# Attention and two feed-forward layers on one core: another way to transpose queries and keys, and other places for the weight splits

## The chip, the core and the metric

The kernel runs on one core of a Trainium2 chip, in one launch. The core has a matrix engine (TensorE; PE in the rows, with its weight loads as PEld), a vector engine (VectorE, DVE), a scalar engine (ScalarE, ACT), a general engine (GpSimd, POOL) and a queue engine (SyncE, SP) that here issues nearly all transfers. Each engine works through its own instructions in the order in which the program gives them, and waits for other engines by semaphores. The metric is the device time of one execution, in microseconds (us). The median of three runs of the kernel before is 856.53 us (856.2 to 856.91).

## The reference

Three stages in float32, each fed by the one before (cut to what matters):

```python
# q, k, v: [4, 8, 576, 64]; a query sees itself and the 63 tokens before it
scores = scale * (q @ k.transpose(0, 1, 3, 2))
mask = (rel >= 0) & (rel < 64)
attn = softmax(where(mask, scores, -1e9))
x = (attn @ v).transpose(0, 2, 1, 3).reshape(2304, 512)
# 8 experts of 288 tokens each, chosen greedily by the logits of x @ w_gate
out[mask_e] = maximum(x[mask_e] @ w1[e], 0) @ w2[e]     # 512 -> 1024 -> 512
# gated layer; its three weights come in float64
g = x @ w_gate2                                          # 512 -> 1536
y = (g * sigmoid(g) * (x @ w_val)) @ w_out               # 1536 -> 512
```

## The kernel before, in words

**Attention.** The 8 heads are taken as 4 pairs, head hp and head hp + 4, so that 128 partitions hold 64 values of d of two heads. A unit is a window of 64 queries of one pair; a pair has 9 units, all 16 pairs (4 batches) have 144, and a group is four units that follow each other, so there are 36 groups. The loop over the groups is written out as a software pipeline: in step i the matrix engine makes the scores of group i (`scores`, a mask matmul and a float32 matmul for each unit), transposes the probabilities of group i - 3 (`transposed`) and multiplies those of group i - 5 with the values (`values`); the vector engine takes the maxima of group i, the scalar engine the exponentials of group i - 1 (`exponents`), and GpSimd divides by the sums (`norms`, `pn`). The scalar engine then moves the results out (`out_x`).

Queries and keys are needed with d on the partitions. Before the change the transfers bring 32 tokens and 32 values of d to a quadrant of 32 partitions (`load_qk`: pieces of 32 float32, 128 bytes), and the vector engine transposes 32 by 32 blocks (`prep_k`, `prep_q`: one instruction for the keys of a pair, two for the queries). Only the first two pairs come in rows of eight tokens and are transposed on the matrix engine (`rows`). Values of the block before are copied to the lower 64 partitions by the vector engine and GpSimd (`prep_v`). A small planner gives each of these steps the latest group at which it may come (`steps`, `todo`, `vtodo`, `loads`).

**Routing.** Six rounds of `step`: matrix engine counts (`cnt`), a test on the vector engine (`sat`), two small matmuls (`low`, `tot`), and then the vector engine and GpSimd make the next candidates (`M`, `U`, `below`, `Us`, `u`, `G`). Beside each round three tiles of x are transposed and stored in DRAM, and `Stream.split` prepares the first expert weights on GpSimd.

**Weights.** All weights are used as two float32r parts whose sum is exact: the scalar engine copies the raw tile to the high part (`whi`), and another engine subtracts it for the low part (`wlo`), half a tile of 128 x 1024 at a time. For the experts' weights one half is subtracted on the vector engine and the other on GpSimd. `need` asks for five tiles ahead, with nine buffers for each part. The gated layer's float64 weights are put together as float32 by their bits: one square on the scalar engine and four vector instructions for half a tile (`convert`, tiles `t` and `sq`), 36 halves in all, loaded and stored by `convert_move`.

**Experts.** For each of 8 experts and 8 steps f: `first` (12 matmuls of 288 columns), the second product of the step before (12 more), up to three pieces of the next expert's rows transposed, and three parts of `convert` (two where a piece was transposed). All conversion is done before the last expert (`convert_rest`).

**Gated layer.** Three groups of 768 tokens, 12 steps f each, two blocks a step: 24 matmuls of 384 columns a block, and then 18 matmuls of 512 columns for the step before (`second`). Two PSUM banks (`psg`) alternate between the gate's product and the value's.

The order of the work on each engine is the order in which the program emits it; nothing reorders it later.

Of the kernel before, what the change touches and what calls it, by code (L numbers as in the profile page):

```python
# [7 lines left out]
F32 = mybir.dt.float32  # L8
# [13 lines left out]
class Stream:  # L22
    """Weights: loaded in float32, split on chip into two float32r parts whose sum is exact."""

    def __init__(self, ctx, tc):
        self.nc = tc.nc
        self.raw = ctx.enter_context(tc.tile_pool(name="wraw", bufs=4))
        self.todo, self.raws, self.parts = [], [], {}
        self.nload = self.nsplit = 0
# [8 lines left out]
    def load(self, upto):  # L38
        while self.nload < min(upto, len(self.todo)):
            key, src = self.todo[self.nload]  # L40
            t = self.raw.tile([128] + list(src.shape[1:]), F32, name="wraw")
            self.nc.sync.dma_start(t, src)
            self.raws.append(t)
            self.nload += 1

    def split(self, upto, engine=None):
        upto = min(upto, len(self.todo))
        self.load(upto + 4)
        while self.nsplit < upto:
            key, _ = self.todo[self.nsplit]  # L50
            t = self.raws[self.nsplit]
            h = self.hi.tile(list(t.shape), F32R, name="whi")
            lo = self.lo.tile(list(t.shape), F32R, name="wlo")
            for s in range(2):
                if len(t.shape) == 3 and t.shape[1] % 2 == 0:
                    m = t.shape[1] // 2
                    sl = (slice(None), slice(s * m, s * m + m))
# [3 lines left out]
            self.parts[key] = (h, lo)  # L61
            self.nsplit += 1


class Kernel:
# [29 lines left out]

    def attention(self, ctx):
# [10 lines left out]
        NR = 3  # L107
        raw_p, kt_p, v_p = pool("raw", NR), pool("kt", 3), pool("vw", 8)
# [9 lines left out]
        nc.gpsimd.iota(iq, pattern=[[2, 64]], base=0, channel_multiplier=-1)  # L118
        nc.vector.tensor_scalar(gt, iq, 0.0, None, op0=OP.is_gt)
# [7 lines left out]
        vone = one.tile([128, 1, 1, 1], F32, name="vone")  # L127
        nc.vector.memset(vone, 1.0)
# [4 lines left out]
        NQ, KL, VL = 5, 2, 5  # L133
        qbds = [one.tile([128, NC, 64, 2], F32, name=f"qbd{i}") for i in range(NQ)]
        for i in range(NQ):
            for s in range(2):
                nc.gpsimd.memset(qbds[i][64 * s:64 * s + 64, :, :, 1 - s], 0.0)
# [4 lines left out]
        # A unit is a window of 64 queries of one pair of heads, hp and hp + HP. A group is four units.  # L142
# [4 lines left out]
        raw, kt, vw = {}, {}, {}  # L147

        def load_qk(b, name, j):
            """On the partitions of a quadrant 32 tokens, and 32 of d."""  # L150
            src = self.k if name == "k" else self.q
            raw[name, b, j] = raw_p.tile([128, 2, S // 32, 32], F32, name="raw" + name)
            for s in range(2):
                for dh in range(2):
                    p0, h = 64 * s + 32 * dh, HP * s + 2 * j
                    nc.sync.dma_start(
                        raw[name, b, j][p0:p0 + 32].rearrange("p h t d -> p (h t) d"),
                        src[b, h:h + 2, :, 32 * dh:32 * dh + 32].rearrange("h (t p) d -> p (h t) d", p=32))

        def load_rows(name, h):  # L160
            src = self.k if name == "k" else self.q
            t = v_p.tile([128, NC, 2, D], F32, name="vw")
            raw[name, h] = t[0:72, 0:8].rearrange("p c s d -> p (c s d)").rearrange("p (s x) -> p s x", s=2)
            for s in range(2):
                nc.sync.dma_start(raw[name, h][:, s], src[0, HP * s + h].rearrange("(p t) d -> p (t d)", t=8))

        def load_v(b, hp):
            vw[b, hp] = v_p.tile([128, NC, 2, D], F32, name="vw")
            for s in range(2):
                nc.sync.dma_start(vw[b, hp][64:128, :, s, :], self.v[b, HP * s + hp].rearrange("(c p) d -> p c d", p=64))  # L170

        def rows(name, h):
            """Keys or queries of pair h of the first batch, transposed on the tensor engine; a partition has 8 tokens,
            and two at a time are transposed."""
            p, n = (ps_t, "ps_t") if name == "k" else (ps_o, "ps_o")
            if name == "k":
                dst = kt[0, 0][:, h].rearrange("r (p t e) -> r e t p", t=4, e=2)
            else:
                dst = qbd(0, h).rearrange("r c i s -> r (c i) s").rearrange("r (p t e) s -> r s e t p", t=4, e=2)
            for s in range(2):  # L180
                sl = slice(64 * s, 64 * s + 64)
                ps = p.tile([128, 4, 72], F32, name=n)
                for t in range(4):
                    nc.tensor.transpose(ps[:, t, :], raw[name, h][:, s, 128 * t:128 * t + 128], self.ident[0:72, 0:72])
                for e in range(2):
                    x = ps[64 * e:64 * e + 64]
                    if name == "k":
                        nc.scalar.activation(dst[sl, e], x, AF.Copy)
                    else:
                        nc.vector.tensor_copy(dst[sl, s, e], x)  # L190

        def prep_k(b, hp):
            if hp % 2 == 0:
                kt[b, hp // 2] = kt_p.tile([128, 2, S], F32, name="kt")
            if b == 0 and hp < 2:
                rows("k", hp)
                return
            nc.vector.transpose(kt[b, hp // 2][:, hp % 2], raw["k", b, hp // 2][:, hp % 2].rearrange("p t d -> p (t d)"))

        def prep_q(b, hp, s):  # L200
            if b == 0 and hp < 2:
                if s == 0:
                    rows("q", hp)
                return
            r = raw["q", b, hp // 2][:, hp % 2].rearrange("p (i e) d -> p i (e d)", e=2)
# [982 lines left out]
```

## Time and profile before

| what | value |
| --- | --- |
| median of 3 runs | 856.53 us |
| span of the profiled execution (first to last instruction) | 854.2 us |
| TensorE busy / VectorE busy | 796.9 us (93%) / 542.7 us (64%) |
| ScalarE busy / GpSimd busy | 383.4 us (45%) / 225.3 us (26%) |
| DMA packets, those under 512 bytes | 137931, 88896 |
| DMA moved | 119.50 MB |
| attention, first scores to the last group's mask matmul | 10.16 to 114.13 us |
| routing, first to sixth count | 125.87 to 154.41 us |
| experts, first product to the gated layer's first | 173.14 to 400.61 us |
| gated layer, to the last scatter | 400.61 to 849 us |

The profile gives no time of its own for the profiled execution but its span; what lies around the span is taken as the difference to the median of the runs, 2.3 us. The busy share is an average over these stages, and each of them has another limit, so that they have to be read one by one. A row of the timeline holds start, duration, engine, line, operation, output, inputs, shape, and in brackets the idle time before it and what ended that. A row of a group holds the same for all instructions of a line, with count, total, mean in ns, and the idle time before.

### The profile page before, as it was taken

The numbers are of one execution on the slowest core, as the hardware profiler recorded it, in microseconds if no ns is written. First come the engines' busy times: TensorE is split into PE (matmuls) and PEld (weight loads), VectorE is DVE, ScalarE is ACT, GpSimd is POOL, SyncE is SP. The second block draws the span as 40 slices with busy tenths as digits, with TensorE's granted clock in tenths as the row PEclk, the third lists the DMA queues.
The fourth block names the chain that finished last, engine by engine and source line by source line (L and its number), as shares of the span: only waits on it lengthen the run. The fifth ranks groups of instructions, "written<-read, shape, count | busy, mean of one in ns | idle before, by whom it ended". The sixth has DMA issues, their size and how long they took to land.

```text
span 854.2 us, 14581 instructions
## 1 busy us (share of the span) xinstructions
PE 796.9 (93%) x5411; PEld 738.6 (86%) x5411; DVE 542.7 (64%) x1014; ACT 383.4 (45%) x980; POOL 225.3 (26%) x263
## 2 busy tenths in 40 slices
PE   5879895499999999999999999999999999999996
PEld 4668774299999999999999999999999999999996
DVE  5868888789999999976443444554344454433422
ACT  4777875356555665666322323433222343221311
POOL 6765745544455444440000000020000002000002
PEclk9999997599999999999999999999999999999998
DMA  9999935679999998855311222241122224101001
GB/s 141 137 142 144 195 113 177 186 243 312 290 318 307 302 315 287 285 187 174 99 29 46 74 74 74 75 149 35 41 74 74 75 74 148 43 32 50 1 1 74
DMA packets 137931, 119.50 MB, mean 140 GB/s; under 512 B 88896, under 2 KB 105280, under 8 KB 137856
## 3 DMA queue, kind: packets, MB, share of 16 engines
q1 hardware_dynamic: 134976, 109.09, 47.2%
q0 software_dynamic: 2880, 9.44, 3.6%
q8 instruction: 44, 0.72, 0.4%
q14 instruction: 31, 0.25, 0.1%
HBM read 99.63 MB, written 18.87 MB: 139 GB/s over the span
## 4 chain that ended last, share of the span: by engine, by line
issue 36%; PE 24%; DVE 16%; POOL 2%; ACT 1%; DMA 0%; POOLq 0%; DVEq 0%; ACTq 0%
PE psg L983 13%; DVE wlo L60 6%; PE pso L983 5%; PE psa L983 3%; PE psw L983 3%; DVE t L940 2%; DVE hl L973 2%; DVE t L938 2%; POOL out_dram L1123 2%; DVE t L936 2%; DVE t L942 1%; DVE xt L976 1%; ACT whi L58 0%; PE psw L1015 0%; DMA w<-t 0%
## 5 line engine op out<-in xcount | busy, mean ns | idle before, releaser
L983 PE MATMUL psg<-y,whi 128*128 128x384 f32 x1152 | 223.1, 336 | 0.0
L983 PEld LDWEIGHTS psg<-y,whi 128*128 128x128 f32 x1152 | 201.6, 188 | 0.0
L1123 POOL DMA_INDIRECT out_dram<-orow,idx x18 | 17.3, 963 | 443.5 <-ACT orow L1121 271.6
L983 PE MATMUL pso<-whi,p 128*128 128x512 f32 x432 | 133.3, 390 | 0.0
L60 DVE TENSOR_TENSOR wlo<-wraw,whi 128x512 fp32r<-128x512 f32 x167 | 129.6, 820 | 4.5 <-ACT whi L58 4.1
L58 ACT ACTIVATE whi<-wraw 128x512 fp32r<-128x512 f32 x236 | 130.4, 620 | 0.1
L60 POOL TENSOR_TENSOR wlo<-wraw,whi 128x512 fp32r<-128x512 f32 x69 | 100.0, 1459 | 103.4 <-ACT whi L58 40.2
L1100 DVE TENSOR_TENSOR sg<-sg,psg 128x384 f32<-128x384 f32 x72 | 39.9, 554 | 131.7 <-ACT sg L1099 131.7
L983 PE MATMUL psg<-y,wlo 128*128 128x384 f32 x576 | 123.4, 336 | 0.0
L1105 ACT ACTIVATE p<-sg 128x384 fp32r<-128x384 f32 x72 | 37.8, 525 | 152.7 <-DVE sg L1103 150.5
L983 PEld LDWEIGHTS psg<-y,wlo 128*128 128x128 f32 x576 | 102.5, 188 | 2.8 <-DVE sg L1100 0.2
L1099 ACT ACTIVATE sg<-psg 128x384 f32<-128x384 f32 x72 | 35.4, 491 | 147.0 <-PE psg L983 147.0
L983 PEld LDWEIGHTS pso<-whi,p 128*128 128x128 f32 x432 | 80.6, 188 | 14.5
L983 PE MATMUL pso<-wlo,p 128*128 128x512 f32 x216 | 84.2, 390 | 0.0
L983 PE MATMUL psa<-hl,whi 128*128 128x288 f32 x256 | 78.4, 306 | 5.2 <-DVE hl L973 4.8
L1103 DVE TENSOR_TENSOR sg<-sg,psg 128x384 f32<-128x384 f32 x72 | 39.9, 554 | 66.5 <-PE psg L983 66.2
L983 PE MATMUL psw<-xt,whi 128*128 128x288 f32 x512 | 78.4, 295 | 0.0
L983 PE MATMUL psa<-hh,whi 128*128 128x288 f32 x256 | 75.4, 295 | 0.0
L983 PE MATMUL psa<-hh,wlo 128*128 128x288 f32 x256 | 75.4, 295 | 0.0
L983 PEld LDWEIGHTS psw<-xt,whi 128*128 128x128 f32 x512 | 71.3, 188 | 0.0
L1106 DVE TENSOR_TENSOR p<-sg,p 128x384 fp32r<-128x384 f32 x72 | 40.2, 559 | 42.6 <-ACT p L1105 42.0
L245 ACT ACTIVATE pp<-ps_s,nm 128x128 f32<-128x128 f32 x144 | 51.0, 369 | 26.8 <-DVE nm L238 24.6
(179 smaller groups left out, 1157.9 us busy)
## 6 DMA issues: line engine op xcount, KB each, us to landing
wraw<-in_moe_w_dram SPq DMA_DIRECT2D x64, 512.0 KB
wraw<-w SPq DMA_DIRECT2D x54, 512.0 KB
w<-t SPq DMA_DIRECT2D x36, 256.0 KB
raw<-in_moe_w_gate_dram SPq DMA_DIRECT2D x12, 512.0 KB
raw<-in_moe_w_val_dram SPq DMA_DIRECT2D x12, 512.0 KB
raw<-in_moe_w_out_dram SPq DMA_DIRECT2D x12, 512.0 KB
vw<-in_v_dram SPq DMA_DIRECT2D x32, 144.0 KB
xrows<-row SPq DMA_DIRECT2D x18, 256.0 KB
```

What stands on the lines that cost most here:

```text
L58: self.nc.scalar.activation(h[sl], t[sl], AF.Copy)
L60: eng.tensor_tensor(lo[sl], t[sl], h[sl].bitcast(F32), op=OP.subtract)
L245: nc.scalar.activation(PP[g][:, u, :], ps[:, u, :], AF.Exp, bias=nm[:, u:u + 1], scale=scale, accum_out=SM[g][:, u:u + 1])
L936: nc.vector.tensor_scalar(t, hi, 0x07FFFFFF, 3, op0=OP.bitwise_and, op1=OP.logical_shift_left)
L938: nc.vector.scalar_tensor_tensor(t, hi, -0x40000000, t, op0=OP.bitwise_and, op1=OP.bitwise_or)
L983: self.nc.tensor.matmul(acc, x, y, start=start and i == 0, stop=stop and i == len(seq) - 1)
L1099: nc.scalar.activation(sg, pg, AF.Sigmoid)
L1100: nc.vector.tensor_tensor(sg, sg, pg, op=OP.mult)
L1103: nc.vector.tensor_tensor(sg, sg, pv, op=OP.mult)
L1105: nc.scalar.activation(p[0][:, sl], sg, AF.Copy)
L1106: nc.vector.tensor_tensor(p[1][:, sl], sg, p[0][:, sl].bitcast(F32), op=OP.subtract)
L1123: d = nc.gpsimd.indirect_dma_start(out=self.out, out_offset=bass.IndirectOffsetOnAxis(ap=self.idx[:, 6 * g + t:6 * g + t + 1], axis=0), in ...
```

## The change

Queries and keys of all pairs now come in rows of two tokens (128 float32, 512 bytes: `load_rows`) on 72 partitions, and the matrix engine transposes them, four transposes into one PSUM bank for each of two heads and for q and k (`prep`). The keys leave PSUM in two copies on the scalar engine, the queries in two on the vector engine, each copy writing every second float32. The scores' operands lie head by head rather than interleaved, and the mask is made accordingly. Values of the block before are copied by a transfer on the chip (`copy_v`). `out_x` moves from the scalar to the vector engine in the loop. The scores have two PSUM banks instead of three, the transposes three instead of two.

No weight is split on GpSimd any more. `Stream.half` splits half a tile, on the scalar and vector engines, and stands in `step` between the counts and `sat` in the first six rounds; after the routing `split(6)` takes the place of six conversion parts. `need` asks for four tiles ahead, with seven buffers. `convert` is called for 10 parts an expert and goes on through the last expert and into the gated layer, four parts after each block; a tile is loaded only once it is stored (`limit`). The comments that the change deletes are left out here.

```diff
+        self.limit = lambda: len(self.todo)
-        self.hi = ctx.enter_context(tc.tile_pool(name="whi", bufs=9))
-        self.lo = ctx.enter_context(tc.tile_pool(name="wlo", bufs=9))
+        self.hi = ctx.enter_context(tc.tile_pool(name="whi", bufs=7))
+        self.lo = ctx.enter_context(tc.tile_pool(name="wlo", bufs=7))
...
-    def split(self, upto, engine=None):
-        upto = min(upto, len(self.todo))
-        self.load(upto + 4)
...
-                self.nc.scalar.activation(h[sl], t[sl], AF.Copy)
-                eng = engine or (self.nc.gpsimd if s and key[0] in ("w1", "w2") else self.nc.vector)
-                eng.tensor_tensor(lo[sl], t[sl], h[sl].bitcast(F32), op=OP.subtract)
...
+    def half(self):
+
+        if self.nsplit == len(self.todo):
+            return
+        self.load(self.nsplit + 5)
...
+        sl = (slice(None), slice(self.nhalf * m, self.nhalf * m + m))
+        self.nc.scalar.activation(h[sl], t[sl], AF.Copy)
+        self.nc.vector.tensor_tensor(lo[sl], t[sl], h[sl].bitcast(F32), op=OP.subtract)
+        self.nhalf = 1 - self.nhalf
+        self.nsplit += not self.nhalf
...
+        NR, NQ, NV, VL = 3, 4, 6, 5
...
-        ps_s, ps_t, ps_o, ps_l = pool("ps_s", 3, PS), pool("ps_t", 2, PS), pool("ps_o", 2, PS), pool("ps_l", 1, PS)
+        ps_s, ps_t, ps_o, ps_l = pool("ps_s", 2, PS), pool("ps_t", 3, PS), pool("ps_o", 2, PS), pool("ps_l", 1, PS)
...
+        def load_rows(name, b, hp):
+
             src = self.k if name == "k" else self.q
-            raw[name, b, j] = raw_p.tile([128, 2, S // 32, 32], F32, name="raw" + name)
+            t = raw[name, b, hp] = raw_p.tile([72, 2, 4, 2 * D], F32, name="raw" + name)
             for s in range(2):
...
+                nc.sync.dma_start(t[:, s], src[b, HP * s + hp].rearrange("(t p e) d -> p t (e d)", p=72, e=2))
...
+        def copy_v(b, hp):
+
+            nc.sync.dma_start(vw(b, hp)[0:64, 1:NC], vw(b, hp)[64:128, 0:NC - 1])
+
+        def prep(name, b, hp, s):
+
+
+            ps = ps_t.tile([128, 4, 72], F32, name="ps_t")
+            for t in range(4):
+                nc.tensor.transpose(ps[:, t, :], raw[name, b, hp][:, s, t], self.ident[0:72, 0:72])
...
+            dst = dst.rearrange("r c (m e) -> r e c m", e=2)
+            for e in range(2):
+                x = ps[64 * e:64 * e + 64].rearrange("r t p -> r (t p)").rearrange("r (c m) -> r c m", c=NC)
+                if name == "k":
+                    nc.scalar.activation(dst[:, e], x, AF.Copy)
+                else:
+                    nc.vector.tensor_copy(dst[:, e], x)
...
-                out_x(i - VL - 1)
+                out_x(i - VL - 1, True)
             take(i)
             if i >= 1:
                 norms(i - 1)
-            for a in vtodo.get(i, ()):
-                prep_v(*a)
...
             def beside(i):
-                self.st.split(i, self.nc.gpsimd)
                 self.store_rows(3)
                 self.convert_move()
...
                 mm(cnt, G[:, c, :], bl[:, c, :], start=c == 0, stop=c == NT - 1)
+            if it < first:
+                self.st.half()
             nc.vector.tensor_scalar(self.sat[0:32], cnt[:, 0:NE], cnt[:, NE:NE + 1], 0.5 - CAP,
...
+        if self.halves:
+            st.limit = lambda: 8 * NE + self.stored // 2 if self.stored < len(self.halves) else len(st.todo)
 
     def need(self, key):
-        self.st.split(self.order[key] + 5)
+        self.st.split(self.order[key] + 4)
...
         self.convert_move()
-        self.convert(6)
+        self.st.split(6)
...
-                n = 3
                 if todo and f % 2 == 0:
                     transposed(*todo.pop(0))
-                    n = 2
-                if e < NE - 1:
-                    self.convert(n)
-                elif f in (1, 4):
+                self.convert(2 if f % 4 == 3 else 1)
+                if e == NE - 1 and f in (1, 4):
                     self.ready(f // 4)
...
+                self.convert_move()
                 block(g, f, p, 0)
+                self.convert()
...
+                self.convert_move()
                 block(g, f, p, 1)
+                self.convert()
```

What this does to the order on the engines is shown at three places. The first is one group in the middle of the attention on the matrix engine, before the change: mask and scores (`ps_s`), transposes of the probabilities (`ps_t`), products with the values (`ps_o`).

```order
L225 LDWEIGHTS identb
L225 MATMUL ps_s<-mask,identb 128x512
L229 MATMUL ps_s<-kt,qbd_143 128x128 x4
L262 MATMUL ps_t<-ident,pn 128x128 x4
L278 MATMUL ps_o<-pt,vw 64x64 x8
```

And a group of the changed kernel at the same stage, `rawq` and `rawk` being the rows of queries and keys of a later pair.

```order
L206 LDWEIGHTS identb
L206 MATMUL ps_s<-mask,identb 128x512
L210 MATMUL ps_s<-kt,qbd_146 128x128 x4
L243 MATMUL ps_t<-ident,pn 128x128 x4
L259 MATMUL ps_o<-pt,vw_156 64x64 x8
L184 MATMUL ps_t<-ident,rawq 128x72 x4
L184 MATMUL ps_t<-ident,rawk 128x72 x4
```

Eight transposes of 72 rows have come to the end of the group; the vector engine's 32 by 32 transposes are gone from its own order.

The second place is the vector engine in two steps of an expert, before: `hl` is the low part of the hidden layer, `wlo` that of a weight, `xt` that of the next expert's rows, and `t` are conversion parts.

```order
L973 SCALAR_TENSOR_TENSOR hl<-psw,hh 128x288
L976 TENSOR_TENSOR xt_5961<-psw,xt_5960 128x4x64
L942 SCALAR_TENSOR_TENSOR t_6015<-sq_6016,t_6015 128x512
L936 TENSOR_SCALAR t_6068<-raw_5941 128x512
L973 SCALAR_TENSOR_TENSOR hl<-psw,hh 128x288
L60 TENSOR_TENSOR wlo<-wraw,whi 128x512
L938 SCALAR_TENSOR_TENSOR t_6068<-raw_5941,t_6068 128x512
L940 SCALAR_TENSOR_TENSOR t_6068<-raw_5941,t_6068 128x512
L942 SCALAR_TENSOR_TENSOR t_6068<-sq_6069,t_6068 128x512
L60 TENSOR_TENSOR wlo<-wraw,whi 128x512
```

The same engine in two steps of an expert of the changed kernel.

```order
L933 SCALAR_TENSOR_TENSOR hl<-psw,hh 128x288
L936 TENSOR_TENSOR xt_6270<-psw,xt_6269 128x4x128
L896 SCALAR_TENSOR_TENSOR t_6393<-raw_1757,t_6393 128x512
L933 SCALAR_TENSOR_TENSOR hl<-psw,hh 128x288
L60 TENSOR_TENSOR wlo<-wraw,whi 128x512 x2
L898 SCALAR_TENSOR_TENSOR t_6393<-raw_1757,t_6393 128x512
L60 TENSOR_TENSOR wlo<-wraw,whi 128x512 x2
```

Four halves of weights stand where two stood, the other two having been on GpSimd, and two conversion parts where five stood.

The third place is the vector engine in the gated layer, where the second step of the first group ends and the third begins, in the changed kernel: `sg` and `p` belong to the block, `t` to the conversion, `wlo` to the next three weight tiles.

```order
L1056 TENSOR_TENSOR sg<-sg,psg 128x384
L1059 TENSOR_TENSOR sg<-sg,psg 128x384
L1062 TENSOR_TENSOR p_9195<-sg,p_9194 128x384
L894 TENSOR_SCALAR t_9273<-raw_9153 128x512
L896 SCALAR_TENSOR_TENSOR t_9273<-raw_9153,t_9273 128x512
L898 SCALAR_TENSOR_TENSOR t_9273<-raw_9153,t_9273 128x512
L900 SCALAR_TENSOR_TENSOR t_9273<-sq_9274,t_9273 128x512
L60 TENSOR_TENSOR wlo<-wraw,whi 128x512 x6
L1056 TENSOR_TENSOR sg<-sg,psg 128x384
```

Before the change no conversion stands here: only the six halves came between the blocks.

## Rows read from the trace of the kernel before

**Rows 1.** Windows: length, then busy us (count) of PE, PEld, DVE, ACT, POOL.

```profile
core 0 of [0], span 854.2 us
66.46:80.30 13.84, 13.74 (x178) 12.03 (x174) 13.34 (x39) 12.89 (x60) 10.68 (x13) 1.00 1.23 141
173.14:400.61 227.47, 222.26 (x1629) 213.81 (x1630) 212.79 (x298) 137.57 (x284) 101.80 (x73) 1.00 0.86 276
```

**Rows 2.** Timeline, PE, attention: first scores, then mask matmuls of three groups.

```profile
10.16 2.04 PE L229 MATMUL ps_s<-kt,qbd 128*128 128x128 f32 x8 [2.44 <-ACT kt L188]
...
66.46 0.39 PE L225 MATMUL ps_s<-mask,identb 128*128 128x512 bf16 x1
...
80.30 0.39 PE L225 MATMUL ps_s<-mask,identb 128*128 128x512 bf16 x1
...
114.13 0.38 PE L225 MATMUL ps_s<-mask,identb 128*128 128x512 bf16 x1
```

**Rows 3.** Groups by line, 0 to 160 us: query transposes and copies out of PSUM.

```profile
L206 DVE STREAM_TRANSPOSE qbd<-rawq 64x576 f32<-64x576 f32 x28 | 21.6, 771 | 12.4 <-DMA rawq<-in_q_dram 12.0
...
L188 ACT ACTIVATE kt<-ps_t 64x288 f32<-64x288 f32 x8 | 5.5, 684 | 4.6 <-PE ps_t L184 4.5
...
L190 DVE COPY qbd<-ps_o 64x288 f32<-64x288 f32 x8 | 5.2, 646 | 1.6 <-PE ps_o L184 1.5
```

**Rows 4.** Timeline, PEld, 13 to 16 us: eight transposes of keys.

```profile
14.31 0.58 PEld L184 LDWEIGHTS ps_t<-ident,vw 72*128 72x128 f32 x8
```

**Rows 5.** Timeline, ACT, one group of the attention.

```profile
67.58 0.37 ACT L245 ACTIVATE pp<-ps_s,nm 128x128 f32<-128x128 f32 x1
...
68.96 0.61 ACT L270 ACTIVATE pt<-ps_t 128x512 f32<-128x512 f32 x1
69.44 0.41 ACT L294 ACTIVATE big<-ps_o 128x256 f32<-128x256 f32 x1
```

**Rows 6.** Groups by line, 195 to 410 us: scalar copy, and the pieces' transposes.

```profile
L972 ACT ACTIVATE hh<-psw 128x288 fp32r<-128x288 f32 x57 | 23.4, 410 | 54.2 <-PE psw L983 53.1 <-issue 1.1
...
L1015 PEld LDWEIGHTS psw<-ident,xg 128*128 128x128 f32 (+3 forms) x80 | 8.2, 139 | 1.5 <-issue 1.3 <-PE psa L983 0.2
```

**Rows 7.** Windows of the instructions on tile t: length, DVE busy (count), clock, DMA.

```profile
168.06:170.67 2.61, 2.43 (x4) 0.51 0.81 209
178.00:378.00 200.00, 113.18 (x136) 1.00 0.91 291
```

**Rows 8.** Timeline, routing: counts on PE, and one round's POOL and DVE.

```profile
125.87 0.90 PE L651 MATMUL cnt<-below,G 128*32 128x9 bf16 x18
...
130.22 0.64 PE L651 MATMUL cnt<-below,G 128*32 128x9 bf16 x18 [1.40 <-DVE G L615]
...
154.41 0.65 PE L651 MATMUL cnt<-below,G 128*32 128x9 bf16 x18 [2.82 <-DVE G L615]
...
132.95 2.48 POOL L60 TENSOR_TENSOR wlo<-wraw,whi 128x512 fp32r<-128x512 f32 x2
...
132.99 2.52 DVE L608 SCALAR_TENSOR_TENSOR Us<-below,U 128x88 f32<-128x88 bf16 x2
```

**Rows 9.** Groups by line and shape, DVE, 178 to 378 us.

```profile
L60 DVE TENSOR_TENSOR wlo<-wraw,whi 128x512 fp32r<-128x512 f32 x56 | 58.9, 1052 | 2.0 <-ACT whi L58 1.9
...
L973 DVE SCALAR_TENSOR_TENSOR hl<-psw,hh 128x288 fp32r<-128x288 f32 x56 | 25.2, 450 | 0.4 <-ACT hh L972 0.2
```

**Rows 10.** The same for 420 to 800 us.

```profile
L60 DVE TENSOR_TENSOR wlo<-wraw,whi 128x512 fp32r<-128x512 f32 x95 | 58.6, 686 | 0.0
L1106 DVE TENSOR_TENSOR p<-sg,p 128x384 fp32r<-128x384 f32 x61 | 34.1, 559 | 36.1 <-ACT p L1105 35.5 <-issue 0.6
```

**Rows 11.** Chain that ended last, in order of time: start, length, what.

```profile
394.24 1.60 PE psa L983 x12
...
421.48 8.32 PE psg L983 x48
429.81 4.09 PE pso L983 x18
```

More of the change, by code (lines that the diff above doesn't have):

```diff
@@ L44, in load, with split @@
             self.nload += 1
-    def split(self, upto, engine=None):
-        upto = min(upto, len(self.todo))
-        self.load(upto + 4)
[L49 to L57, printed above, removed]
-                self.nc.scalar.activation(h[sl], t[sl], AF.Copy)
-                eng = engine or (self.nc.gpsimd if s and key[0] in ("w1", "w2") else self.nc.vector)
-                eng.tensor_tensor(lo[sl], t[sl], h[sl].bitcast(F32), op=OP.subtract)
-            self.parts[key] = (h, lo)
-            self.nsplit += 1
+    def half(self):
+        if self.nsplit == len(self.todo):
+            return
+        self.load(self.nsplit + 5)
+        key, _ = self.todo[self.nsplit]
+        t = self.raws[self.nsplit]
+        if key not in self.parts:
+            self.parts[key] = [p.tile(list(t.shape), F32R, name=n) for p, n in ((self.hi, "whi"), (self.lo, "wlo"))]
+        h, lo = self.parts[key]
+        m = t.shape[1] // 2
+        sl = (slice(None), slice(self.nhalf * m, self.nhalf * m + m))
[3 more added lines that the diff above has]
+        self.nsplit += not self.nhalf
+    def split(self, upto):
+        while self.nsplit < min(upto, len(self.todo)):
+            self.half()
 class Kernel:
@@ L117, in attention @@
         iq = one.tile([128, 64], I32, name="iq")
-        nc.gpsimd.iota(iq, pattern=[[2, 64]], base=0, channel_multiplier=-1)
-        nc.vector.tensor_scalar(gt, iq, 0.0, None, op0=OP.is_gt)
+        nc.gpsimd.iota(iq, pattern=[[1, 64]], base=0, channel_multiplier=0)
+        place = one.tile([128, 2], I32, name="place")
+        nc.gpsimd.iota(place[:, 0:1], pattern=[[1, 1]], base=0, channel_multiplier=1)
+        nc.vector.tensor_scalar(place[:, 1:2], place[:, 0:1], 63, None, op0=OP.bitwise_and)
+        num = one.tile([128, 1], F32, name="num")
+        nc.vector.tensor_copy(num, place[:, 1:2])
+        nc.vector.tensor_scalar(gt, iq, num, None, op0=OP.is_gt)
         nc.vector.tensor_scalar(mask[:, 4, 64:128], gt, big, None, op0=OP.mult)
@@ L180, in rows @@
[L180 to L205, printed above, removed]
-            nc.vector.transpose(qbd(b, hp)[64 * s:64 * s + 64, :, :, s], r[64 * s:64 * s + 64])
@@ L382, in attention @@
         for i in range(NG - 1):
-            for at, x in loads:
-                if at == i:
-                    load(x)
+            for h in loads.get(i, ()):
+                load(h)
             scores(i)
@@ L499, in build @@
         self.st.open(self.ctx, tc)
-        self.xg_p, self.xg = self.conv.enter_context(tc.tile_pool(name="xg", bufs=4, side="right")), {}
+        self.xg_ctx = ExitStack()
+        self.xg_p, self.xg = self.xg_ctx.enter_context(tc.tile_pool(name="xg", bufs=4, side="right")), {}
         with ExitStack() as ctx:
@@ L897, in weights_setup @@
             self.pieces[key] = t
-    def convert_rest(self):
-        while self.stored < len(self.halves):
-            self.convert_move()
-            self.convert()
-        self.conv.close()
     def convert_move(self, queue=None):
```

140 lines of the change are left out of this document (52 added, 88 removed).

## The prediction

> **What bounds the kernel now.** I read the slices of the page first, then windows, timelines and groups of one stage at a time, and the chain of waits last. The average says little: four stages have four limits.
>
> In the attention the transfers are full: even in the best stretch, 66.46 to 80.30 us, their share is 1.23, and the matrix engine is busy for 13.74 of 13.84 us [rows 1]. The six groups of that stretch take 2.31 us each; over all 35 periods, 10.16 to 114.13, the mean is 2.97 [rows 2]. The difference, 23 us in all, is stalls; the vector engine's query transposes alone wait 12.0 us for their rows [rows 3]. So the stage has two limits close together: transfers, and right behind them a matrix engine at 2.31.
>
> In the routing the first round takes 4.35 us and the next four 24.19, 6.05 each [rows 8]. What differs is that GpSimd subtracts two weight halves from the second round on: both stand for 2.48 us, and the vector engine's `Us` pair, begun 0.04 us later, for 2.52 [rows 8].
>
> In the experts the vector engine is busy for 212.8 of 227.5 us and the matrix engine waits for it at the end of the chain [rows 1]. There a `wlo` takes 1.05 us; where GpSimd is silent it takes 0.69 [rows 9, 10]. A conversion part takes 0.83 against 0.61 [rows 7].
>
> In the gated layer the chain is the matrix engine alone: 48 matmuls for 8.32 us and 18 for 4.09, step after step, 12.41 in all [rows 11].
>
> **Attention.** Removed are the vector engine's transposes, the copies of values and nearly three quarters of the small packets, so I take the transfer stalls to be gone. Added on the matrix engine are 16 transposes for each of the 14 pairs that had none: 224 at 0.0725 us (0.58 for eight) [rows 4], 16.2 us. Its floor is 35 x 2.31 + 16.2 = 97 us. The scalar engine has the exponentials of a group, 67.58 to 68.96, 1.38 us, and the copy `pt`, 0.48 to the next start [rows 5], and now 64 key copies over 36 groups in the place of `out_x`. The price of such a copy isn't in the trace: today it is 0.684 us writing every eighth float32 [rows 3]; 288 contiguous columns cost 0.41 [rows 6]. The new copies write every second. The conversion reads every second word at 0.61 us for 512 [rows 7], no slower than contiguous, so I take a value near the contiguous end, 0.45, and keep 0.684. That gives 2.66 a group, under the matrix engine's 2.77; with 0.684 it is 3.08, 108 us.
>
> [...]
>
> The new wait is the second bank of scores: scores of group i + 2 wait for the exponentials of group i, and these for two query copies that come behind the transposes at the group's end. With 2.77 to these, 0.9 for the copies and 1.38 for the exponentials the loop holds two groups for 5.05 us, 2.5 each, inside the floor. On SP a value copy stands in front of later loads and waits only for a load given one pair earlier. I take 101 us, the floor and 4 for engines that wait for each other: 3 us gained, ends -7 and +4.
>
> **Routing.** Without GpSimd's halves the five intervals would take 5 x 4.35 = 21.8 us instead of 28.54. A half on the vector engine stands in front of `sat` instead, 0.69 us, partly beside the counts: up to 3.4 us over five rounds, of which I take 2.5, since in the first round it also waits for the scalar engine. Gain 4.3, ends 3.4 and 6.8. After the routing six halves replace six parts on the vector engine at about the same price: nothing.
>
> **Experts.** A step is 24 matmuls, 3.20 us (1.60 for twelve) [rows 11], 64 steps 204.8; 23 pieces of four transposes at 0.10 (8.2 us for 80) [rows 6] add 9.4. Floor 214.2 against 227.5 now. The vector engine needs for a step 0.45 for `hl` [rows 9], two halves at 0.69 [rows 10], 1.25 parts at 0.61, and at most 0.25 for `xt` (23 at no more than 0.69 in 64 steps): 2.84, under the matrix engine's 3.35. Between the `hl` of an odd step and that of the next stand four halves and one or two parts, 3.4 to 4.0 us; a hidden half is needed only a product later, so this jitter is covered. I take 11.5 gained, 1.8 short of the floor for the start and for the last expert, which now also converts. Ends 5 and 13.3.
>
> **Gated layer.** Moved here are 16 halves of conversion, 64 parts in the first eight steps. A step costs the vector engine six instructions at 0.56 [rows 10], three halves and eight parts, 3.4 + 2.1 + 4.9 = 10.4 of 12.41 us. It fits, but not evenly: at the end of every second step come four parts and six halves in one piece, 2.4 + 3.7 to 4.1, before the next block's first product can be taken out of its bank. Counted from the start of such a step: parts of the first block until 8.5, the second block's three instructions until 10.7, parts until 13.2, halves until 17.1, the product's bank free at 17.7; the next product wants that bank at 12.41 + 4.16 = 16.6. That is 1.1 us of stall, four times, and some for the tokens split in the seventh step: 5 us lost, ends 0 and 12.
>
> **Sum.** 854.2 - 3 - 4.3 - 11.5 + 5 = 840.4 for the span; the runs' median lies 2.3 us above the span, so 842.7, rounded to 842.5.
>
> **Rivals.**
> Nothing stalls (828): attention at its floor, -7, routing -6.8, experts -13.3, gated 0: -27 gives 829.4, and the start of the attention can give 1 more. For it: the matrix engine ran at 99% in the best stretch. Against: the three other engines come within 10% of its period.
>
> Dear copies (852): at 0.684 the scalar engine sets 3.08 a group, and the query copies at 0.646 lengthen the loop. Attention 108 plus 3 for waits, +7: 852.5. For it: the only rows of this copy. Against: their step was 32 bytes and more.
>
> The vector engine stays slow, the other side (about 892): the long `wlo` and parts in the experts would be due to the full transfers there (share 0.86 [rows 1]), not to GpSimd. Then a step costs 0.45 + 2 x 1.05 + 1.25 x 0.83 + 0.25 = 3.84 us, 246 over 64, 18.5 more than now. In the gated layer the pieces of four parts grow by 0.9 each and the six halves by 2.2, so that the stall of 1.1 becomes 4 to 5 us, four times, 18 to 20. With 3 gained in the attention and nothing in the routing: 854.2 - 3 + 18.5 + 20 + 2.3 = 892. It decides from 0.95 us a half, where the step passes 3.35. Against: the `Us` pair that ends with GpSimd's pair [rows 8]. [...]
>
> That the change doesn't do what it says is no rival here: the orders show the moves.
>
> **How the numbers follow.** My forecast, 836 to 848 by itself, 0.55; nothing stalls 0.2; dear copies 0.17; slow vector engine 0.05; 0.03 for a loss beyond 12 us in the gated layer, which would end near today's time. The range 828 to 853 leaves out the last two and the edges. A measurement of this kernel tells 0.2%, 1.7 us, from no change: faster by more 0.91, within it 0.03, slower 0.06.
>
> **What would show it.** Attention periods near 2.9 with the matrix engine over 90% busy and no wait for `rawq`; key copies near 0.45. Rounds of about 4.8 us and short `Us`. In the experts `wlo` at 0.69, the vector engine near 85% and the matrix engine above 97%. In the first eight gated steps four gaps of about 1 us before `psg`, none later. Wrong if the experts still take over 222 us, if the attention takes over 106, or if the gated layer's gaps reach 2 us.

## The result, and the profile after

The changed kernel takes 841.48 us (median of four runs, 840.74 to 843.68) against 856.37 for the kernel before (856.04 to 856.91): a ratio of 0.9829, interval [0.9815, 0.9843]. The forecast was 842.5. The profiled execution has a span of 839.0 us, 15.2 less than before.

| stretch | before | after | difference | forecast |
| --- | --- | --- | --- | --- |
| start to first count | 125.87 | 123.96 | -1.9 | -3 |
| first to sixth count | 28.54 | 22.73 | -5.8 | -4.3 |
| sixth count to the experts' first product | 18.73 | 17.79 | -0.9 | 0 |
| experts | 227.47 | 215.38 | -12.1 | -11.5 |
| gated layer to the end of the span | 453.6 | 459.1 | +5.5 | +5 |

The windows of the changed kernel show the limits (length, then busy time and count of PE, PEld, DVE, ACT and POOL, then clock, DMA share and GB/s). They answer to [rows 1]: the first is the same 14 us of the attention, the second the whole attention from first to last mask, the third the experts, the fourth the first nine gated steps.

```profile
66.46:80.30 13.84, 13.30 (x176) 12.13 (x176) 10.31 (x35) 13.66 (x58) 5.67 (x6) 1.00 0.96 205
9.47:112.56 103.09, 98.83 (x1196) 87.31 (x1195) 74.96 (x244) 91.01 (x366) 39.03 (x55) 0.97 0.93 201
164.48:379.86 215.38, 215.38 (x1629) 212.96 (x1630) 162.50 (x295) 127.58 (x266) 12.31 (x14) 1.00 0.74 239
379.86:493.61 113.75, 109.39 (x577) 101.59 (x577) 86.55 (x149) 43.71 (x84) 0.00 (x0) 1.00 0.53 174
```

In the experts TensorE no longer idles at all. In the gated layer it now idles for 4.4 us, where it idled for none before. In the attention it is busy for 96%, and ScalarE for 88%.

Groups by line, 0 to 160 us, give the price of the new copies, which [rows 3] did not have (busy us and mean ns of one; then the idle time before, and what ended it):

```profile
L196 ACT ACTIVATE kt<-ps_t 64x288 f32<-64x288 f32 x64 | 27.5, 430 | 12.5 <-PE ps_t L184 11.8
...
L198 DVE COPY qbd<-ps_t 64x288 f32<-64x288 f32 x64 | 29.3, 457 | 8.5 <-PE ps_t L184 7.8
```

0.43 and 0.457 us: near the taken 0.45. What is left of TensorE's waiting is in the view of waits, 9 to 113 us (total us, times, longest); no row names `rawq` any more, and the wait for `rawk` ends before the first mask matmul:

```profile
PE ps_s L206 <- ACT pp L226: 4.1, 8, 0.9
...
PE ps_t L184 <- DMA rawk<-in_k_dram: 1.2, 1, 1.2
```

The counts of the rounds and two of TensorE's waits for `sat` between them, to be set beside [rows 8], and VectorE's `Us` pair:

```profile
123.96 0.90 PE L613 MATMUL cnt<-below,G 128*32 128x9 bf16 x18
126.24 0.16 PE L620 MATMUL low<-sat,w 33*128 33x8 bf16 x1 [1.38 <-DVE sat L616]
129.31 0.63 PE L613 MATMUL cnt<-below,G 128*32 128x9 bf16 x18 [1.40 <-DVE G L577]
...
139.61 0.16 PE L620 MATMUL low<-sat,w 33*128 33x8 bf16 x1 [1.30 <-DVE sat L616]
...
146.69 0.65 PE L613 MATMUL cnt<-below,G 128*32 128x9 bf16 x18 [1.15 <-ACT whi L59]
```

```profile
132.16 0.41 DVE L570 SCALAR_TENSOR_TENSOR Us<-below,U 128x88 f32<-128x88 bf16 x2
```

The pair takes 0.41 us where it took 2.52. In the experts the low halves are short too (groups, 178 to 378 us, against [rows 9]):

```profile
L60 DVE TENSOR_TENSOR wlo<-wraw,whi 128x512 fp32r<-128x512 f32 x119 | 76.9, 688 | 2.5 <-ACT whi L59 0.7
L933 DVE SCALAR_TENSOR_TENSOR hl<-psw,hh 128x288 fp32r<-128x288 f32 x60 | 27.3, 455 | 23.4 <-ACT hh L932 22.6
```

And the chain that ended last, in the gated layer (start, length, what), which in [rows 11] was TensorE alone:

```profile
428.87 3.69 DVE wlo L60 x6
...
433.08 4.44 PE psg L943 x24
...
454.88 3.70 DVE wlo L60 x6
...
459.09 4.43 PE psg L943 x24
```

Every second step six halves stand in the chain, and the block behind them is late.

### The profile page after: what moved, and what is told of

Read it like the earlier page. It is cut to its first block, busy times and chain, and to the rows that moved or that the text cites. A ratio compares the mean times of both kernels' runs of the same rounds, so it can differ in the third digit from the quotient of the medians.

```text
span 839.0 us, 14875 instructions
## 1 busy us (share of the span) xinstructions
PE 801.5 (96%) x5635; PEld 750.0 (89%) x5635; DVE 516.9 (62%) x1104; ACT 396.3 (47%) x998; POOL 94.9 (11%) x167
## 4 chain that ended last, share of the span: by engine, by line
PE 38%; issue 33%; DVE 6%; POOL 2%; ACT 1%; DMA 1%; POOLq 0%; DVEq 0%
PE psw L943 12%; PE psa L943 12%; PE psg L943 9%; PE pso L943 4%; DVE wlo L60 2%; POOL out_dram L1079 1%; PE psw L975 1%; DVE t L898 1%; DVE t L896 1%; DVE sg L1059 1%; DVE t L900 1%; ACT p L1061 1%; DVE sg L1056 1%; DVE t L894 0%; DMA wraw<-in_moe_w_dram 0%
## 5 line engine op out<-in xcount | busy, mean ns | idle before, releaser
L60 DVE TENSOR_TENSOR wlo<-wraw,whi 128x512 fp32r<-128x512 f32 x236 | 149.7, 687 | 8.8 <-DVEq L674 3.8
L943 PE MATMUL psa<-hl,whi 128*128 128x288 f32 x256 | 75.5, 295 | 0.0
L932 ACT ACTIVATE hh<-psw 128x288 fp32r<-128x288 f32 x64 | 26.3, 411 | 61.8 <-PE psw L943 60.5
```

What stands on the lines that cost most here:

```text
L60: self.nc.vector.tensor_tensor(lo[sl], t[sl], h[sl].bitcast(F32), op=OP.subtract)
L932: nc.scalar.activation(h, x, AF.Relu)
L943: self.nc.tensor.matmul(acc, x, y, start=start and i == 0, stop=stop and i == len(seq) - 1)
```

## The experiments

Each is the changed kernel with the edit shown, cut to what matters. The ratios are to the kernel before on the same chip; three chips were used, and it took 855.75, 856.13 and 856.00 us there.

**GpSimd back in the experts.** The copy to the high part stays on ScalarE; the low part of every second half goes to GpSimd from the first expert on.

```diff
-        self.nc.vector.tensor_tensor(lo[sl], ...)
+        eng = self.nc.gpsimd if self.pooled and self.nhalf and key[0] in ("w1", "w2") else self.nc.vector
+        eng.tensor_tensor(lo[sl], ...)
```

> The changed kernel, but in the experts the low part of every second half of a weight is made by GpSimd again, as before the change; the thin conversion stays. Theory (room): the experts gained because VectorE's work for a step fell below TensorE's 3.35 us; with the thin conversion there is room either way. One of the two halves' 0.69 us leaves VectorE, and if the other pieces slow to what they took beside GpSimd before ([rows 9]: 1.05 us a half), VectorE has 0.45 + 1.05 + 1.25 x 0.83 + 0.25 = 2.8 us a step. TensorE stays the bound: experts 215 to 217 us, total 841 to 843 us, with VectorE's half at 0.8 to 1.05 us. Rival (GpSimd alone): taking the splits off GpSimd is what paid, and it comes back: experts towards 227 us, total about 853 us.

842.19 us, ratio 0.9836 [0.9808, 0.9865]; experts 165.2 to 381.3, 216.1 us. The groups of the experts, 165 to 381 us, of VectorE and of GpSimd:

```profile
L62 DVE TENSOR_TENSOR wlo<-wraw,whi 128x512 fp32r<-128x512 f32 x64 | 68.0, 1067 | 3.9 <-ACT whi L60 2.1
...
L898 DVE SCALAR_TENSOR_TENSOR t<-raw,t 128x512 int32<-128x512 int32 x20 | 21.0, 1050 | 0.1
```

```profile
L62 POOL TENSOR_TENSOR wlo<-wraw,whi 128x512 fp32r<-128x512 f32 x58 | 95.8, 1664 | 81.0 <-DVE hl L935 56.6 <-ACT whi L60 24.2
```

VectorE's pieces become half as long again while the DMA share (0.72) is that of the changed kernel (0.74): GpSimd makes the long rows, not the transfers. But with the thin conversion TensorE hardly waits for them (busy for 215.5 of 216.1 us), and the time stays. The rival falls.

**Thick conversion back.** Three parts a step, two where rows are transposed; it ends before the last expert.

```diff
-                self.convert(2 if f % 4 == 3 else 1)
+                self.convert(3 if f % 2 or not moved else 2)
```

> The changed kernel, but with the conversion as thick as before: three and two parts a step in the experts, so that it ends there and the gated layer has none; the splits stay on VectorE. Theory (room): some 2.6 parts a step at 0.62 us, two halves at 0.69, 0.45 for hl and 0.25 for what else is there give 3.7 us a step against TensorE's 3.35, so that some 55 steps get 0.3 us longer: experts about 232 us. The gated layer gets back the 5.5 us that it lost: about 453.6 us. Total 841.5 + 17 - 5.5 = 853 us (848 to 856). Rival (GpSimd alone): the experts stay at 215 to 217 us with the thick conversion too, and the total is about 836 to 838 us.

837.30 us, ratio 0.9785 [0.9755, 0.9815], and not 853. The theory fell. The windows of the first seven experts, all experts, and the first gated steps, and VectorE's low halves in the first window:

```profile
164.60:353.00 188.40, 188.40 (x1426) 185.99 (x1427) 178.22 (x328) 118.55 (x246) 12.55 (x13) 1.00 0.90 309
...
164.60:379.80 215.20, 215.20 (x1628) 212.78 (x1629) 197.85 (x359) 136.30 (x282) 12.64 (x14) 1.00 0.86 294
379.80:493.50 113.70, 113.70 (x613) 107.83 (x612) 50.42 (x87) 35.91 (x70) 0.00 (x0) 1.00 0.21 70
```

```profile
L60 DVE TENSOR_TENSOR wlo<-wraw,whi 128x512 fp32r<-128x512 f32 x105 | 67.6, 685 | 0.6
```

VectorE is busy for 178.2 of 188.4 us and TensorE's busy time has no gap. 178.2 over 56 steps is 3.18 us a step, where the sum by rows had been 3.7. Two things were wrong in that sum. It charged two halves a step, and 105 came in 56 steps. And the rows overlap: counts times means of all groups of this stretch add up to 198.3 us, 20.1 more than the busy time, 61 ns for each of 328 instructions. The row also answers the transfers once more: at a DMA share of 0.90, as full as before the change (0.86), a half without GpSimd takes 0.685 us. The gated layer takes 453.3 us, 5.8 less than in the changed kernel.

**Both back.** The two edits together.

> The changed kernel with both edits of the experts undone: the thick conversion (three and two parts a step, none left for the gated layer), and the second halves of the experts' splits on GpSimd. With either alone undone the experts took 216.1 us (GpSimd back) and 215.2 us (thick conversion back), against 215.4 in the changed kernel and 227.5 before. Theory (either edit is enough, both undone is too much): VectorE's work beside GpSimd is 0.45 + 1.07 + 2.6 x 0.94 + 0.25 = 4.2 us by the rows of the run with GpSimd back, more than TensorE's 3.35; experts 225 to 230 us, gated layer 453.3, total 841.5 + 12 - 6 = 847.5 us (845 to 850). Rival: what held the experts before was something else that the change also altered (splits in one burst of a weight, look-ahead of five, nine buffers); then the experts stay under 219 us, and the total is 836 to 839 us.

849.17 us, ratio 0.9927 [0.9903, 0.9951]; experts 166.2 to 394.4, 228.2 us. The window of the first 188.8 us of the experts, the wait over all experts, and the same wait in the kernel before (173 to 400 us):

```profile
166.20:355.00 188.80, 184.01 (x1348) 176.41 (x1349) 182.00 (x257) 112.74 (x233) 86.63 (x63) 1.00 0.88 293
```

```profile
PE psa L945 <- DVE hl L935: 5.8, 14, 0.9
```

```profile
PE psa L983 <- DVE hl L973: 4.8, 15, 0.7
```

VectorE is at 96% and TensorE waits for `hl`, as before the change. VectorE's 182.0 us over the 52 steps that the window holds by its count of `hl` are 3.5 us a step, above TensorE's 3.35; the 4.2 by rows was too high once more. That completes a square (experts / gated layer, us):

| | thin conversion | thick conversion |
| --- | --- | --- |
| splits on VectorE | 215.4 / 459.1 | 215.2 / 453.3 |
| every second half on GpSimd | 216.1 / 459.2 | 228.2 / 453.2 |

With the rest of the change in place, either edit alone brings the experts to TensorE's floor; the second one gains nothing more there, and the thin conversion has a price of 5.8 to 6.0 us in the gated layer.

**The same, side by side.** The changed kernel and the one with the thick conversion once more, on one chip.

> The changed kernel itself, beside the three that follow on the same chip. Both theories: 841 to 842.5 us, 0.983 of the kernel before.

> The changed kernel with the thick conversion, as in the run before that had it, on the same chip as the changed kernel. Theory (with the splits off GpSimd the thin conversion buys nothing in the experts and costs the gated layer 5.9 us): 4 to 6 us less than the changed kernel, 836 to 837.5 us. Rival (the run before was a lucky one): within 2 us of the changed kernel.

842.16 us, 0.9838 [0.9824, 0.9851], and 836.19 us, 0.9771 [0.9757, 0.9784]: 6.0 us apart, and the intervals don't touch. The version with the thin conversion left out beats both kernels.

**The gated layer's halves one by one.** A half is split behind each block and behind each second product; the same two lines go around the second block.

```diff
+                self.st.load(self.st.nsplit + 5)
                 block(g, f, p, 0)
                 self.convert()
+                self.st.half()
...
                     second(*late.pop(0))
+                self.st.half()
```

> The changed kernel, but in the gated layer the six halves of weights that fell into one burst every second step are split one by one, behind each half-step and behind each second product, and a piece is loaded a half-step sooner. Theory (bursts): the 5.9 us that the gated layer lost (459.2 against 453.3 with no conversion in it) come from six splits and four parts of conversion in a row ahead of sg's product on VectorE; spread, the queue ahead of it is at most one split and four parts, and the loss falls under 1.5 us: gated layer 453.5 to 455, total 836 to 838 us. Rival (conversion as such): four parts of 0.62 us stand ahead of the sg product in every half-step, or the pieces arrive late; the gated layer stays at 457 us or more, total 839.5 us or more.

843.10 us, ratio 0.9863 [0.9835, 0.9892]; gated layer 379.8 to 840.3, 460.5 us. No gain: the rival's number, but not quite its mechanism. The chain that ended last:

```profile
395.66 4.43 PE psg L943 x24
400.10 4.09 PE pso L943 x18
404.19 8.32 PE psg L943 x48
412.51 4.09 PE pso L943 x18
...
465.70 1.47 ACT y L935 x2
467.17 0.53 ACT whi L59
467.71 0.68 DVE wlo L60
468.39 1.74 DVE y L936 x2
470.13 0.60 DVE wlo L60
470.73 0.48 DVE sg L1056
471.25 4.43 PE psg L943 x24
```

From 395.66 to 458 TensorE runs without a gap, through two of the places where the changed kernel's burst had made a block late (407 and 433 us). So the bursts are the cause there. But the first two steps now stall for longer (TensorE busy 22.41 of the first 25.20 us, against 24.22 in the changed kernel), and a new stall of 0.83 us stands at 471 us, where the split tokens `y` of the next block stand in the same queue as the halves. Two more come at 547 and 697 us (0.87 and 1.38 us), where the changed kernel has none. There a copy of finished rows (`orow`) waits for an output transfer, and a half stands behind it, ahead of `sg`:

```profile
545.06 0.69 DVE L1075 COPY orow<-pso 128x512 f32<-128x512 f32 x1 [3.72 <-DMA out_dram<-orow,idx]
545.67 0.68 DVE L60 TENSOR_TENSOR wlo<-wraw,whi 128x512 fp32r<-128x512 f32 x1
```

In all TensorE waits for 5.9 us, 4.4 in the changed kernel: what the spread gave it lost at these places.

**The old attention in the changed kernel.** The whole function `attention` is that of before.

> The changed kernel with the attention of before (queries and keys in blocks of 32 tokens, transposed on VectorE). Theory: the attention's part of the gain is the 1.9 us of its own stretch and nothing of it reaches the stages behind: total 841.5 + 1.9 = 843.4 us (842 to 845), with the first count at 125.9 us. Rival 1: the attention's transposes gave nothing by themselves (within 0.8 us of 841.5). Rival 2: the attention also carries part of the routing's gain (its end with fewer transfers under way), and the total is 846 us or more.

845.41 us, ratio 0.9866 [0.9836, 0.9896], between theory and second rival. The first count comes at 126.75 us, 2.8 later. Another 3.6 us lie between it and the experts, and there the clock differs. Windows of the changed kernel and of this one, first to sixth count and on to the experts:

```profile
124.00:147.20 23.20, 14.20 (x184) 12.31 (x183) 19.72 (x83) 14.34 (x38) 6.45 (x20) 0.81 0.64 216
147.20:164.50 17.30, 8.02 (x75) 5.07 (x72) 11.19 (x32) 6.68 (x18) 7.21 (x8) 0.57 0.55 166
```

```profile
126.80:151.70 24.90, 17.46 (x182) 15.34 (x182) 19.14 (x82) 14.18 (x38) 6.61 (x20) 0.57 0.56 201
151.70:170.90 19.20, 8.41 (x76) 5.16 (x73) 12.05 (x33) 7.42 (x20) 8.31 (x8) 0.57 0.53 158
```

The granted clock falls to 0.50 in the rounds in both (132 to 136 us); in the changed kernel it is back at 1.00 between 140 and 144 us, here it is still 0.50 then. The execution of this kernel with the highest mean clock, 0.979, took 843.66 us, and three of the changed kernel at 0.980 and 0.981 took 840.74 to 841.68: 2.0 to 2.9 apart. I take the attention at 2 to 3 us; whether its end also makes the clock fall is open.

**The routing's splits back on GpSimd.** A whole weight behind each round instead of a half in front of `sat`, its low part on GpSimd; the experts' splits stay on VectorE.

```diff
             def beside(i):
+                self.st.split(i)
...
-            if it < first:
-                self.st.half()
```

> The changed kernel, but in the rounds of the routing a whole weight is split behind each round, with its low part on GpSimd, as before the change. Theory: the rounds go back from 22.7 us between the first and the sixth count towards 28.5, and the step after them by 1 us: total 841.5 + 5.8 + 0.9 = 848 us (845.5 to 849). In the trace the halves of Us, or of oh, that fall beside GpSimd's subtraction take over 1 us. Rival: the rounds are shorter for another reason (fewer bytes in small transfers, the attention's end), and the total stays within 1.5 us of 841.5.

846.98 us, ratio 0.9887 [0.9858, 0.9916], +5.5; first to sixth count 123.34 to 151.95, 28.6 us. One round of GpSimd and of VectorE:

```profile
130.39 2.48 POOL L62 TENSOR_TENSOR wlo<-wraw,whi 128x512 fp32r<-128x512 f32 x2
```

```profile
130.43 2.52 DVE L573 SCALAR_TENSOR_TENSOR Us<-below,U 128x88 f32<-128x88 bf16 x2
```

The pair of [rows 8] is back to the hundredth, and with it all of the 5.8 us.

**Idle products in the rounds.** On the kernel with the thick conversion.

```diff
             def beside(i):
                 self.store_rows(3)
+                self.warm(self.row_ps.tile([128, 512], F32, name="rowps"), 2)
```

> The kernel with the thick conversion, and two idle products (128x512, bf16) on TensorE in each round of the routing, behind the transposes of the rows. In the profiled executions so far the granted clock falls to 0.5 inside the rounds, for 5 us in the changed kernel (first to sixth count 22.7 us) and from 132 us on in the one with the old attention (24.4 us). Theory (the clock costs the rounds 1 to 3 us): with TensorE busy between, the clock stays at 1.0 longer, the rounds take 20.5 to 22 us and the total is 1 to 2.5 us under the kernel with the thick conversion. Rival: the idle products (0.4 us each at full clock, 0.63 at half) stand ahead of the counts, and the rounds get 1 to 5 us longer.

835.72 us, 0.9759 [0.9744, 0.9773], against 836.19 without: no difference that the intervals tell. First to sixth count took 22.8 us. The clock fell all the same, and earlier: 0.50 between 128 and 132 us, where it was 0.91 in the first profile of the thick conversion and 0.92 in the changed kernel's. The theory wasn't tested, since the clock wasn't held.

**Banks as before.** Three for scores, two for transposes.

```diff
-        ... pool("ps_s", 2, PS), pool("ps_t", 3, PS), ...
+        ... pool("ps_s", 3, PS), pool("ps_t", 2, PS), ...
```

> The changed kernel with three banks for scores and two for transposes, as before the change (the change made it two and three). Theory: the 4.1 us that the score products wait for the exponentials of the group before the last one go, and the attention gets 2 to 4 us shorter: first count at 120 to 122 us instead of 124.0. Rival: with two banks for the transposes of queries, keys and probabilities the wait moves there (TensorE at the transposes, for the copies on ScalarE or VectorE), and the first count is at 124 us or later.

856.00 us in one execution; first count at 136.3 us, 12.3 later. The rival was right. TensorE's groups, 9 to 113 us:

```profile
L184 PE MATMUL ps_t<-ident,rawk 72*128 72x72 f32 x116 | 14.0, 247 | 10.0 <-ACT pt L251 8.8 <-issue 1.1
L206 PE MATMUL ps_s<-mask,identb 128*128 128x512 bf16 x31 | 12.3, 398 | 0.0
```

The wait before the mask is gone, and the key transposes wait 8.8 us for `pt` to leave their bank.

**Dense key copies.**

```diff
-                    kt[b, hp] = kt_p.tile([128, NC, 64], F32, name="kt")
+                    kt[b, hp] = kt_p.tile([128, 2, NC, 32], F32, name="kt")
...
+                k = kt[b, hp].rearrange("p e c m -> p (c m) e")
```

> The changed kernel, but the two copies of transposed keys write consecutive words (even tokens, then odd ones), and the score products read the keys at a stride of 288 words. Prices the stride of 8 bytes in the copies: ScalarE's key copy takes 0.34 to 0.40 us instead of 0.431 (a dense one of 128x512 takes 0.606, so 0.34 by its elements). Theory (TensorE bounds the attention: 98.8 busy of 103 us): the first count moves by less than 1 us from 124.0. Rival 1 (ScalarE, 90.5 busy of 103, bounds it): 60 copies give back 2 to 5 us. Rival 2: reading keys at a stride costs TensorE, and the score products take longer than 0.282 us each.

846.28 us in one execution; first count at 127.7. The groups, 9 to 113 us, of TensorE and ScalarE:

```profile
L209 PE MATMUL ps_s<-kt,qbd 128*128 128x128 f32 x272 | 43.9, 306 | 0.0
```

```profile
L195 ACT ACTIVATE kt<-ps_t 64x288 f32<-64x288 f32 x60 | 24.3, 405 | 8.4 <-PE ps_t L184 7.0
```

The copy falls from 0.431 to 0.405 us, not to the expected 0.34 to 0.40, and the stride moves to TensorE, whose score products go from 282 to 306 ns. Over 288 of them those 24 ns are 6.9 us, more than the 3.7 by which the first count is late; the wait for the exponentials gave part of it back (2.3 us, 4.1 in the changed kernel). A little work taken off ScalarE bought nothing, and work added to TensorE made the stage longer: TensorE bounds it.

**Half of the key copies on VectorE.** On the kernel with the thick conversion: only the first of the two stays on ScalarE.

```diff
-                if name == "k":
+                if name == "k" and not e:
                     nc.scalar.activation(dst[:, e], x, AF.Copy)
```

> The kernel with the thick conversion, and the second of the two copies of each transposed key tile on VectorE instead of ScalarE (30 of 60 copies of 0.43 us; ScalarE was busy 91.5 of the attention's 104 us, VectorE 75.4). Theory: ScalarE stands behind the 4.1 us that the score products wait for exponentials; relieved by 13 us, the wait falls under 2.5 us and the first count comes at 122 to 123.5 us instead of 124.0; total 1 to 2 us under the kernel with the thick conversion. Rival: VectorE's queue gets longer (89 of 104 us) and the row maxima, for which the exponentials wait, come later; the first count is at 124 us or later, total the same or up to 3 us more.

845.84 us, ratio 0.9882 [0.9867, 0.9897], 9.6 more than without; first count at 132.7. The rival again. Waits, 9 to 113 us:

```profile
ACT pp L226 <- DVE nm L219: 23.0, 27, 1.4
...
PE ps_s L206 <- ACT pp L226: 7.5, 15, 1.5
DVE kt L198 <- ACT kt L196: 7.4, 21, 1.9
```

ScalarE is busy for only 72.8 of 104 us and waits 23.0 for the maxima (3.8 in the changed kernel). VectorE, at 83.5, holds them up while it waits for ScalarE's copy of the same tile. The wait that it was to shorten is nearly twice as long.

## Why the prediction was right, step by step

**Experts.** Size and limit were right: 12.1 for 11.5, TensorE at 100% for "above 97%", `wlo` 0.69. VectorE is at 75% instead of 85: its sum of 2.84 a step is 2.54 as measured (162.5 over 64), since it added rows that overlap (counts times means of the changed kernel's groups there give 2.80). The prediction took the two edits as one gain; the square shows that either suffices.

**The vector engine stays slow.** Its 0.05 was not too low: GpSimd alone brings the long rows, at the same DMA share: 1.07 us a half for 0.69, and the `Us` pair ends with GpSimd's, 0.08 us behind it, in both kernels that have it. Not every vector instruction got longer: `wlo`, which has both its inputs in SBUF, did; `hl` reads one of its two from PSUM and kept its time, 452 ns beside GpSimd and 455 without.

**Routing.** 5.8 us came where 4.3 were taken. The mechanism was right; the term that was mis-sized is the round without a half, taken as the first one of before, 4.35 us. Rounds measured 5.35, 4.03, 4.31, 4.99 and 4.05 us. The half in front of `sat` did cost what was taken, though not 0.5 in each round: TensorE waits for `sat` for 1.38, 0.40, 0.59, 1.30 and 0.39 us, where it waited for 0.38 and then four times for 0.31, 2.4 us more in all against 2.5. In the first and fourth round the half waits for ScalarE; in the others it lies beside the counts. Without these 2.4 us a round is 4.06 on average. A first round is longer: its counts take 0.90 us, later ones 0.63 to 0.66. The 0.9 us behind the sixth count were not in the sum.

**Attention.** Stalls on transfers went (12.0 us for `rawq` to none), the copies cost what was taken, and TensorE's transposes cost about what was counted. Yet from first to last mask it is 103.1 us, 2.94 a group: 2 more than the 101 taken, and counted from the first scores, as [rows 2] has it, 102.7 where it was 104.0. TensorE stands still for 4.3 us of it, near the 4 that the sum left for engines that wait for each other. But 4.1 of these, in eight groups, are the loop over the two banks of scores, which the prediction had put "inside the floor": that step failed, and the allowance hid it. The 2 us are in the floor itself. TensorE's own work is 98.8 us and not 97, since the best stretch, from which 2.31 was read, holds none of the three rounds of logits:

```profile
53.99 1.07 PE L283 MATMUL ps_l<-big,wgp 128*32 128x512 f32 x8
...
57.80 0.66 PE L295 MATMUL ps_l<-ident,lt 128*128 128x128 f32 x4
```

To the next product they take 1.0 and 0.5 us, 4.5 in all; part of it comes back in the first groups, which have no probabilities to transpose yet. A group with neither stall nor logits took 2.81 to 2.87 us, against a floor of 2.77 by the sum. Neither a third bank, since the transposes need theirs more, nor half of the key copies on VectorE gave the time back; both cost 9 us and more.

**Gated layer.** +5.5 for +5, and the mechanism is that of the working: six halves behind four parts. For the working's four gaps of 1.1 us the trace has four of 0.66 to 0.91 behind the bursts, 3.4 us in all, the last at 485 us. About 1 us more lies in two waits of the first two steps, where the chain goes through conversion parts and the store of a converted tile; the sum did not have that, so that two small errors cancel in part. None comes later, as predicted.

## What to carry to other kernels

When a change makes two edits against one bottleneck, price each alone: here either brought the stage to its floor, and the second only carried work into a stage that had no room. Before an engine's queue is called too long, take its busy time over a stretch, not the sum of its rows. Where a stage runs near the limit of one engine and another comes within a tenth of it (98.8 and 91.0 us here), look at where a bank or a copy is taken from: in both trials here the wait that was to go showed up, larger, elsewhere.

## What the runs showed of the hardware

- VectorE's neighbours in time overlap in the profile: 328 instructions of 198.3 us by counts and means were 178.2 us of busy time, 61 ns each (first seven experts, thick conversion).
- A copy out of PSUM that writes every second float32 costs little: 0.431 us for 64x288 on ScalarE against 0.405 dense; at every eighth it had been 0.684 [rows 3].
- A float32 product that reads its moving operand at a stride (288 words between neighbours) costs TensorE more: 306 ns for 282.
- Beside GpSimd, VectorE's instructions on SBUF alone got longer (means of the experts with GpSimd back, and of the changed kernel: `wlo` 1067 ns for 688, the four of a conversion 704 to 1050 for 420 to 686), not `hl`, which reads PSUM (452 for 455): one `hl` took 0.45 us in the middle of a GpSimd pair (254.37 us in the kernel with GpSimd back in the experts, the pair 252.07 to 255.59), while the `wlo` in front of it took 1.79.
- GpSimd's time varies too: its half takes 1.24 us in the routing (a pair in 2.48), and in the experts 1.48 (both edits back) and 1.66 us (GpSimd alone back). Why is not shown.
- The granted clock fell in the rounds in every kernel whose windows were read there (means of 0.57 to 0.81 over the rounds), down to 0.50 over 4 us in the changed kernel and in those with the old attention, the thick conversion and the idle products. In the changed kernel it fell between 128 and 132 us (0.92, then 0.50 over the next 4), after TensorE had been busy for 2.40 of the 4 us before and 3.75 of the 4 before those. Two idle products a round did not prevent it (0.50 between 128 and 132 us).
